# An attention and two-layer kernel on one core: the plain block's elementwise chain given to the scheduler ahead of other work, three steps' PSUM banks, and input differences on VectorE

## The chip, the cores and the metric

The kernel runs on one core of a Trainium2 chip. The metric is the device time of one execution in microseconds (us); the kernel before has been timed three times, and a profiled execution was taken besides. Engines are named as in the profile: PE is TensorE (PEld its weight loads), ACT is ScalarE, DVE is VectorE, POOL is GpSimd, SP is the engine that only issues transfers. A small q behind a name (SPq) marks the engine's queue of issued transfers and waits.

## What is computed

Three layers follow one another on 2304 tokens of width 512. The attention has 4 batches, 8 heads, 576 positions and 64 columns a head, half of the heads with a local mask and half with a strided one. Cut to what matters:

```python
x = attention(q, k, v)                    # (2304, 512)
h = x @ w_in                              # first block, 512 -> 2048 -> 512
x = (h - tanh(h)) @ w_out
rms = sqrt(mean(x * x) + 1e-6)            # second block, 512 -> 1536 -> 512
xn = x / rms * rms_g
g, val = xn @ w_gate, xn @ w_val
out = (silu(g) * val) @ w_out2
```

## The kernel before, in words

**Numbers in two parts.** Every float32 matrix is split into a high part that TensorE takes in its fp32r form and the rest as a low part, and each product is three matmuls: high by high, high by low, low by high. A split is two instructions: a copy (ACT), which rounds to the high part, and a subtraction (DVE), which gives the low part. Weights arrive as 64-bit words in tiles called `raw`, and are turned into float32 by ACT (L184 and L186) and a merge on DVE (L196, tile `ct`), and then split: copy L203 on ACT, subtraction L207 on DVE.

**Order of work.** Attention and the first block share the first 460 us: units of `pe_h`, tanh, `pe_x`, and attention in between. The last of the five token groups of the first block carries the conversion of the second block's first 18 weight tiles. Its result is evacuated by `evac_x` (ACT, L890) to DRAM.

The second block is done in two manners. The first 256 tokens (R0) are *plain*: for each of 12 slices f of the 1536 columns, `pe_gv(0, f)` does a gate group and a val group of 12 matmuls each (256 columns, output tiles `ps_h` and `ps_m`), then silu on ACT (L934), the product on DVE (L935), and the split of the product p: copy on ACT (L937), subtraction on DVE (L938). Two slices later `pe_o` multiplies p by the slice's w_out2 (6 matmuls) and adds to two banks of `ps_x`. While this goes on, the remaining weights are loaded, converted and stored to DRAM for later, so the block is both a computation and the preparation of the next.

The other 2048 tokens go through stages in two rounds of 1024 (j), with a pair of slices to a stage (p). There the work of a 2x2 block product is done with 7 products in place of 8, over sums and differences of the inputs (`conv`, tiles `xt`) and of the weights (`Decode`, POOL, lines L302, L285, L286). `conv(m)` makes one of seven inputs: for four of them a difference is formed first (`comb`, L1024, on POOL, 128x1024), and then it is split (copy L1043 on ACT, subtraction L1044 on DVE). For the first round the `conv` calls stand in the plain block, together with the end of the RMS norm (`prep_s`, L966 to L1010), which advances through a generator, three steps to a slice. For the second round they stand in the last stage of the first.

**What sets the order.** A scheduler orders the instructions of each engine before the run, by priority (the order in which the program issues them) and by its own estimate of when each can start. Every engine then takes its instructions in that order, and waits where one is not ready. Two things are fixed by hand: SP's transfers in the second block stand in program order, and so do PE's matmuls after the plain block. In the plain block PE's order is the scheduler's.

**Banks.** PSUM has eight tiles of 128x512 here: `ps_h` h0 and h1, `ps_m` m0 and m1, and four of `ps_x`. In the plain block steps alternate between h0 and h1 for the gate and m0 and m1 for the val. The norm's sum `ps_r` (read by ACT at L995) takes a tile of `ps_m` too. `pe_o` holds two of `ps_x` until the block ends. In the stages after it, the first products take h0, h1, m0 and m1, and `ps_q` and `ps_o` take `ps_x`.

**The loop of the plain block**, for each f: `st2.to(...)` loads and converts weights ahead (load L175 into three `raw` tiles, L184 to L207), `store.plain` and `store.to` store them (L343: `v<-ct`, L362: `w<-w`), `pe_gv(0, f)`, three steps of the generator, `decode.to(...)` from f = 5 on, and `pe_o(0, f - 2)`.

Of the kernel before, what the change touches and what calls it, by code (L numbers as in the profile page):

```python
# [7 lines left out]
F32 = mybir.dt.float32  # L8
F32R = mybir.dt.float32r
# [4 lines left out]
ACTF = mybir.ActivationFunctionType  # L14
ALU = mybir.AluOpType
# [5 lines left out]
WS = 2.0 ** -8  # L21
# [13 lines left out]
def attn_moe_moe_kernel(  # L35
# [24 lines left out]
    nc = tc.nc  # L60
# [6 lines left out]
    scale = 1.0 / float(D) ** 0.5  # L67
# [13 lines left out]
    def runs(s):  # L81

        r = []
        for i, (b, t) in enumerate(subs[s]):
            if r and r[-1][0] == b and r[-1][1] + r[-1][2] == t:
                r[-1][2] += 64
            else:
                r.append([b, t, 64, 64 * i])
        return r
# [36 lines left out]
    for s in range(len(subs)):  # L126
        if len(runs(s)) > 1 or s in LANES:
            _, t0, n, _ = runs(s)[0]
# [6 lines left out]
    def nth(tag, n):  # L135

        turn[tag] = (turn.get(tag, -1) + 1) % n
        return f"{tag}{turn[tag]}"
# [7 lines left out]
    def bank_x(name):  # L146
        return ps_x.tile([128, 512], F32, tag="x", name=name)

    def mm(out_, lhsT, rhs, start, stop):
        nc.tensor.matmul(out_, lhsT, rhs, start=start, stop=stop, skip_group_check=True)  # L150
# [182 lines left out]
    class Store:  # L333


        n = m = 0
# [586 lines left out]
    def pe_gv(j, f):  # L923
        r, n = [], R0
        for kd, pool, tag in (("gate", ps_h, "h"), ("val", ps_m, "m")):
            ps = pool.tile([128, 512], F32, tag=nth(tag, 2), name="ps_" + tag)[:, :n]
            w, x = w2[kd, f].t, xn[j]
            seq = [(a, e, c) for c in range(4) for a, e in ((0, 0), (0, 1), (1, 0))]
            for i, (a, e, c) in enumerate(seq):
                mm(ps, w[:, a, c, :], x[:, e, c, :], i == 0, i == len(seq) - 1)  # L930
            r.append(ps)
            if kd == "gate":
                s = pb.tile([128, n], F32, tag="s", name="s")
                nc.scalar.activation(out=s, in_=ps, func=ACTF.Silu, scale=WS)  # L934
        nc.vector.scalar_tensor_tensor(out=s, in0=r[1], scalar=WS, in1=s, op0=ALU.mult, op1=ALU.mult)  # L935
        t = pb.tile([128, 2, n], F32R, tag="p", name="p", bufs=3)
        nc.scalar.copy(out=t[:, 0], in_=s)  # L937
        nc.vector.tensor_tensor(out=t[:, 1], in0=s, in1=t[:, 0].bitcast(F32), op=ALU.subtract)  # L938
        p_of[j, f] = t

    def pe_o(j, f):
# [74 lines left out]
    def conv(m):  # L1016

        x = xt["raw"]
        b = {(k, h): x[:, 2 * k:2 * k + 2, HT * h:HT * (h + 1)] for k in range(2) for h in range(2)}

        def comb(name, p, q, out=None):
            if out is None:
                out = tmp[0].tile([128, 2, 512], F32, tag="w", name="tr")[:, :, :HT]
            nc.gpsimd.tensor_tensor(out=out, in0=p, in1=q, op=ALU.subtract)  # L1024
            xt[name] = out
            return out

        if m == 1:
            v = b[0, 0]
        elif m == 2:  # L1030
            v = b[1, 0]
        elif m == 3:
            v = b[1, 1]
        elif m == 5:
            v = comb("t1", b[0, 1], b[0, 0])
        elif m == 6:
            v = comb("t2", b[1, 1], xt.pop("t1"))
        elif m == 7:
            v = comb("t3", b[1, 1], b[0, 1])
        else:  # L1040
            v = comb("t4", b[1, 0], xt["t2"], xt["t2"])
        t = xt[m]
        nc.scalar.copy(out=t[:, 0], in_=v)  # L1043
        nc.vector.tensor_tensor(out=t[:, 1], in0=v, in1=t[:, 0].bitcast(F32), op=ALU.subtract)  # L1044
# [310 lines left out]
    pb = poolB.enter_context(tc.tile_pool(name="pb", bufs=2, reuse_waits="tile"))  # L1355

    for f in range(FB):
        if f == FB - 4:
            pairs[0].fetch((0, 1))
        st2.to(max(3 * (f + 2), N1 + (len(w2_order) - N1) * (f + 1) // (FB - 2)))  # L1360
        store.plain(st2.i - 1)
        store.to(st2.i - 6)
        pe_gv(0, f)
        for _ in range(3 if f < FB - 2 else 40):
            next(pg, None)
        decode.to(max(0, min(8, 8 * (f - 4) // 6)))
        if f > 1:
            pe_o(0, f - 2)
# [155 lines left out]
```

## Time and profile before

| what | value |
|---|---|
| median of three runs | 894.25 us (894.15 to 897.34) |
| profiled execution | 893.28 us |
| its span in the trace | 891.5 us |
| granted clock over the span | 0.99 |
| busy: PE, DVE, ACT, POOL | 97%, 71%, 46%, 30% |

The span runs from the first to the last instruction of the program; the profiled execution's own time includes what lies around it. Busy shares are means over parts with different limits, so the table of stretches among the rows below is read beside them. A matmul's end is modelled, so two groups may overlap by a little in the list of instructions; the distance between their starts is the better measure. An entry like "4.8 <-ACT s L934" names the idle time and what ended it.

### The profile page before, as it was taken

How to read it: one execution, taken by the hardware profiler on the slowest of the kernel's cores; microseconds unless marked ns; L12 is line 12 of the kernel's file. 1: busy time of each engine (PE TensorE's matmuls, PEld its weight loads, DVE VectorE, ACT ScalarE, POOL GpSimd, SP SyncE). 2: the span in 40 equal slices, each digit the busy share in tenths (PEclk: the TensorE clock that was granted, in tenths of full speed). 3: DMA queues.
4: the chain of work that ended last, by engine and by line, in shares of the span. 5: the costliest groups of instructions: out<-in, count | busy, mean ns of one | idle time of the engine just before them, and what ended most of it. 6: DMA issues, size and time to landing. Idle time of an engine off the chain costs nothing.

```text
span 891.5 us, 14064 instructions
## 1 busy us (share of the span) xinstructions
PE 866.0 (97%) x5091; PEld 723.4 (81%) x5091; DVE 633.5 (71%) x1282; ACT 413.3 (46%) x915; POOL 271.0 (30%) x317
## 2 busy tenths in 40 slices
PE   6999999999999999999988899999999999999998
PEld 3888888888998887888877887888788888888886
DVE  5999788888689896658869935469678553435544
ACT  6887643233444234868767534533325324322230
POOL 0000147694285952000003759846213000000000
PEclk9999999999999999999998999999999999999999
DMA  9964224311313102899958699865562189544002
GB/s 323 352 223 171 78 78 143 110 49 42 109 59 103 42 1 88 302 323 384 408 182 309 230 340 379 318 230 213 201 202 69 57 319 358 187 145 139 1 1 94
DMA packets 63750, 164.12 MB, mean 184 GB/s; under 512 B 10113, under 2 KB 21761, under 8 KB 63681
## 3 DMA queue, kind: packets, MB, share of 16 engines
q1 hardware_dynamic: 62528, 162.18, 51.6%
q10 hardware_dynamic: 1152, 1.05, 0.4%
q8 instruction: 40, 0.66, 0.3%
q14 instruction: 30, 0.24, 0.1%
HBM read 119.16 MB, written 44.04 MB: 183 GB/s over the span
## 4 chain that ended last, share of the span: by engine, by line
PE 58%; DVE 10%; POOL 7%; issue 2%; ACT 2%; DMA 2%; SPq 0%; DVEq 0%; ACTq 0%; POOLq 0%
PE ps_pr L150 20%; PE ps_o L150 14%; PE ps_x L150 9%; PE ps_h L150 9%; POOL pr L674 5%; DVE so L714 4%; PE ps_q L150 4%; PE ps_m L150 1%; POOL pr L707 1%; DVE tg L859 1%; DVE g L870 1%; DMA w<-w 1%; DMA wt<-w 1%; POOL ws L302 0%; DVE sm L450 0%
## 5 line engine op out<-in xcount | busy, mean ns | idle before, releaser
L150 PE MATMUL ps_h<-xs,w 128*128 128x512 f32 (+1 forms) x984 | 214.3, 366 | 0.7 <-DVE tg L859 0.7
L150 PE MATMUL ps_x<-g,w 128*128 128x512 f32 (+1 forms) x984 | 214.5, 366 | 0.2 <-ACT g L865 0.2
L150 PEld LDWEIGHTS ps_h<-xs,w 128*128 128x128 f32 x984 | 169.9, 190 | 30.6 <-DVE tg L859 1.1
L150 PEld LDWEIGHTS ps_x<-g,w 128*128 128x128 f32 x984 | 168.4, 189 | 30.5 <-ACT g L865 0.6
L150 PE MATMUL ps_pr<-xt,wt 128*128 128x512 f32 x576 | 137.4, 390 | 1.5 <-DVE s L1084 0.5
L150 PE MATMUL ps_o<-wt,p 128*128 128x512 f32 x576 | 135.9, 389 | 0.0
L150 PEld LDWEIGHTS ps_pr<-xt,wt 128*128 128x128 f32 x576 | 107.7, 188 | 25.7 <-DVE v L1096 1.4
L150 PEld LDWEIGHTS ps_o<-wt,p 128*128 128x128 f32 x576 | 108.1, 188 | 22.5
L674 POOL TENSOR_TENSOR pr<-sk,sq 128x256 f32<-128x256 f32 (+2 forms) x101 | 82.7, 856 | 132.0 <-DMA sq<-in_q_str_dram 126.7
L865 ACT CAST g<-tg 128x512 fp32r<-128x512 f32 (+1 forms) x82 | 46.5, 567 | 100.5 <-DVE tg L859 100.4
L1103 ACT COPY u<-ps_pr 128x512 f32<-128x512 f32 x72 | 41.9, 587 | 102.4 <-PE ps_pr L150 102.4
L707 POOL TENSOR_TENSOR pr<-sv,se 128x288 f32<-128x288 f32 (+12 forms) x104 | 69.9, 695 | 56.4 <-DVE so L714 19.8
L1154 DVE SCALAR_TENSOR_TENSOR osum<-ps_o,osum 128x512 f32<-128x512 f32 x80 | 54.6, 687 | 26.5 <-PE ps_o L150 26.2
L714 DVE TENSOR_REDUCE so<-pr 128x16 f32<-128x272 f32 (+11 forms) x104 | 65.3, 653 | 8.5 <-POOL pr L707 8.1
L150 PE MATMUL ps_pr<-xt,wo 128*128 128x512 f32 x288 | 67.4, 389 | 0.0
L1024 POOL TENSOR_TENSOR tr<-x 128x1024 f32<-128x1024 f32 x4 | 11.8, 2948 | 176.1 <-DMA raw<-in_w_val_dram 140.8
L150 PEld LDWEIGHTS ps_pr<-xt,wo 128*128 128x128 f32 x288 | 54.1, 188 | 11.3
L870 DVE TENSOR_TENSOR g<-tg,g 128x512 fp32r<-128x512 f32 (+1 forms) x82 | 54.9, 671 | 10.4 <-ACT g L865 9.8
L196 DVE SCALAR_TENSOR_TENSOR ct<-ca,ct 128x512 uint32<-128x512 uint32 x68 | 49.1, 731 | 18.6 <-ACT ca L186 18.1
L859 DVE SCALAR_TENSOR_TENSOR tg<-ps_h,tg 128x512 f32<-128x512 f32 (+1 forms) x82 | 50.6, 619 | 14.9 <-ACT tg L854 14.8
L854 ACT ACTIVATE tg<-ps_h 128x512 f32<-128x512 f32 (+1 forms) x82 | 44.2, 541 | 36.2 <-PE ps_h L150 36.2
L207 DVE TENSOR_TENSOR w<-ct,w 128x512 fp32r<-128x512 f32 x68 | 49.5, 737 | 11.2 <-ACT w L203 11.2
(122 smaller groups left out, 1077.2 us busy)
## 6 DMA issues: line engine op xcount, KB each, us to landing
wt<-w SPq DMA_DIRECT2D x84, 512.0 KB, 4.5
w<-w SPq DMA_DIRECT2D x36, 512.0 KB, 6.8
raw<-in_w_out_dram SPq DMA_DIRECT2D x28, 512.0 KB, 6.4
w<-wo SPq DMA_DIRECT2D x24, 512.0 KB, 6.8
raw<-in_w_in_dram SPq DMA_DIRECT2D x16, 512.0 KB, 9.0
raw<-in_w_gate_dram SPq DMA_DIRECT2D x12, 512.0 KB, 7.6
raw<-in_w_val_dram SPq DMA_DIRECT2D x12, 512.0 KB, 7.1
v<-ct SPq DMA_DIRECT2D x24, 256.0 KB, 6.3
```

What stands on the lines that cost most here:

```text
L150: nc.tensor.matmul(out_, lhsT, rhs, start=start, stop=stop, skip_group_check=True)
L196: nc.vector.scalar_tensor_tensor(out=t, in0=self.a.bitcast(U32), scalar=3, in1=t, op0=ALU.logical_shift_left, op1=ALU.bitwise_or)
L207: eng.tensor_tensor(out=t[:, 1], in0=self.b, in1=t[:, 0].bitcast(F32), op=ALU.subtract)
L674: nc.gpsimd.tensor_tensor(out=pr, in0=self.k[:, a:e, :], in1=self.q[:, c - c0:c - c0 + 1, :].to_broadcast([128, e - a, D]), op=ALU.mult,)
L707: nc.gpsimd.tensor_tensor(out=pr, in0=self.v[:, 0:c + 1, a:e], in1=self.e[:, c - c0, 0:c + 1].unsqueeze(2).to_broadcast([128, c + 1, e - a ...
L714: pend.append(lambda: nc.vector.tensor_reduce(out=o[:, c - g0, a:e], in_=pr.rearrange("l c d -> l d c"), axis=AX.X, op=ALU.add))
L854: nc.scalar.activation(out=t, in_=h_of[g, f, a], func=ACTF.Tanh, scale=WS)
L859: nc.vector.scalar_tensor_tensor(out=t, in0=h_of.pop((g, f, a)), scalar=WS, in1=t, op0=ALU.mult, op1=ALU.subtract)
L865: nc.scalar.copy(out=t[:, 0], in_=t_of[g, f, a])
L870: nc.vector.tensor_tensor(out=t[:, 1], in0=t_of.pop((g, f, a)), in1=t[:, 0].bitcast(F32), op=ALU.subtract)
L1103: nc.scalar.copy(out=u, in_=x[kd])
L1154: nc.vector.scalar_tensor_tensor(out=o, in0=ps, scalar=WS, in1=o, op0=ALU.mult, op1=ALU.add)
```

## The change

In `pe_gv` the tiles of every third step (f = 2, 5, 8, 11) come from `ps_x`, not from `ps_h` and `ps_m`, and the counters of those two don't advance in that step. The silu, which was issued behind the gate group, is now issued behind both groups, and it, the product, the copy and the subtraction stand in a block of higher priority: the scheduler treats them as if they had been issued 400 places earlier. Tile `s` has three buffers in place of two. In `conv`, the difference of two inputs is formed on DVE in place of POOL; `conv` is used for both rounds, so eight instructions in all move, four in the plain block and four in the last stage of the first round.

```diff
@@ pe_gv @@
         for kd, pool, tag in (("gate", ps_h, "h"), ("val", ps_m, "m")):
-            ps = pool.tile([128, 512], F32, tag=nth(tag, 2), name="ps_" + tag)[:, :n]
+            if f % 3 == 2:
+                ps = bank_x("ps_" + tag)[:, :n]
+            else:
+                ps = pool.tile([128, 512], F32, tag=nth(tag, 2), name="ps_" + tag)[:, :n]
...
-            if kd == "gate":
-                s = pb.tile([128, n], F32, tag="s", name="s")
-                nc.scalar.activation(out=s, in_=ps, func=ACTF.Silu, scale=WS)
-        nc.vector.scalar_tensor_tensor(out=s, in0=r[1], scalar=WS, in1=s, op0=ALU.mult, op1=ALU.mult)
-        t = pb.tile([128, 2, n], F32R, tag="p", name="p", bufs=3)
-        nc.scalar.copy(out=t[:, 0], in_=s)
-        nc.vector.tensor_tensor(out=t[:, 1], in0=s, in1=t[:, 0].bitcast(F32), op=ALU.subtract)
+        with tc.high_priority(400):
+            s = pb.tile([128, n], F32, tag="s", name="s", bufs=3)
+            nc.scalar.activation(out=s, in_=r[0], func=ACTF.Silu, scale=WS)
+            nc.vector.scalar_tensor_tensor(out=s, in0=r[1], scalar=WS, in1=s, op0=ALU.mult, op1=ALU.mult)
+            t = pb.tile([128, 2, n], F32R, tag="p", name="p", bufs=3)
+            nc.scalar.copy(out=t[:, 0], in_=s)
+            nc.vector.tensor_tensor(out=t[:, 1], in0=s, in1=t[:, 0].bitcast(F32), op=ALU.subtract)
@@ conv, comb @@
-            nc.gpsimd.tensor_tensor(out=out, in0=p, in1=q, op=ALU.subtract)
+            nc.vector.tensor_tensor(out=out, in0=p, in1=q, op=ALU.subtract)
```

## Rows read from the trace of the kernel before

**Rows 1.** The page, part 1: busy time, share of the span, instructions of each engine.

```profile
PE 866.0 (97%) x5091; PEld 723.4 (81%) x5091; DVE 633.5 (71%) x1282; ACT 413.3 (46%) x915; POOL 271.0 (30%) x317
```

**Rows 2.** Stretches: length, busy PE, PEld, DVE, ACT, POOL, granted clock, DMA share, GB/s.

```profile
464.00:472.00 8.00, 1.70 (x13) 1.49 (x12) 7.00 (x10) 7.97 (x12) 0.00 (x0) 0.85 0.81 255
472.00:477.20 5.20, 5.00 (x26) 5.00 (x27) 4.36 (x10) 3.97 (x10) 0.00 (x0) 0.57 0.92 297
477.20:491.00 13.80, 13.80 (x96) 12.67 (x95) 13.39 (x15) 8.23 (x15) 7.39 (x3) 1.00 0.89 336
491.00:497.00 6.00, 3.67 (x16) 3.38 (x16) 6.00 (x9) 3.92 (x7) 0.62 (x1) 0.72 0.37 113
497.00:518.00 21.00, 21.00 (x149) 19.72 (x149) 17.51 (x21) 9.40 (x20) 20.33 (x16) 1.00 0.85 284
518.00:528.00 10.00, 9.05 (x47) 7.46 (x46) 2.54 (x5) 3.60 (x8) 1.60 (x2) 1.00 0.99 342
528.00:560.00 32.00, 31.05 (x136) 25.02 (x135) 15.70 (x19) 13.56 (x24) 30.80 (x34) 1.00 0.99 372
560.00:891.50 331.50, 327.36 (x1441) 269.84 (x1439) 196.07 (x269) 108.73 (x179) 57.19 (x51) 1.00 0.47 167
```

**Rows 3.** Who PE waited for, 450 to 640 us: total, times, longest.

```profile
PE ps_h L150 <- ACT s L934: 4.8, 1, 4.8
PE ps_x L150 <- DVE p L938: 2.3, 1, 2.3
PE ps_m L150 <- ACT acc L995: 1.7, 1, 1.7
```

**Rows 4.** PE in order of time: start, length, operation, count, idle before.

```profile
472.20 4.98 PE L150 MATMUL ps_h<-xn,w 128*128 128x256 f32 x24 [4.84 <-ACT s L934]
...
503.79 1.59 PE L150 MATMUL ps_h<-xn,w 128*128 128x256 f32 x12
505.22 1.60 PE L150 MATMUL ps_m<-xn,w 128*128 128x256 f32 x12
...
523.47 1.59 PE L150 MATMUL ps_m<-xn,w 128*128 128x256 f32 x12
```

**Rows 5.** ACT in order of time, 455 to 500 us.

```profile
460.68 1.09 ACT L890 ACTIVATE xe<-ps_x 128x512 f32<-128x512 f32 x2 [2.89 <-PE ps_x L150]
...
470.47 1.28 ACT L934 ACT_TABLE_LOAD   x1
```

**Rows 6.** DVE and POOL in order of time, 455 to 521 us.

```profile
466.73 1.22 DVE L1044 TENSOR_TENSOR xt<-x,xt 128x1024 fp32r<-128x1024 f32 x1
...
481.30 4.88 DVE L1010 SCALAR_TENSOR_TENSOR x<-x,gcol,sq 128x512 f32<-128x512 f32 x4
...
486.77 2.60 DVE L196 SCALAR_TENSOR_TENSOR ct<-ca,ct 128x512 uint32<-128x512 uint32 x1
489.30 3.41 DVE L1044 TENSOR_TENSOR xt<-x,xt 128x1024 fp32r<-128x1024 f32 x1
...
493.30 0.68 DVE L196 SCALAR_TENSOR_TENSOR ct<-ca,ct 128x512 uint32<-128x512 uint32 x1
...
500.45 2.55 DVE L207 TENSOR_TENSOR w<-ct,w 128x512 fp32r<-128x512 f32 x1
...
482.84 2.79 POOL L1024 TENSOR_TENSOR tr<-x 128x1024 f32<-128x1024 f32 x1 [140.85 <-DMA raw<-in_w_val_dram]
...
497.60 4.86 POOL L1024 TENSOR_TENSOR tr<-x,tr 128x1024 f32<-128x1024 f32 x1 [5.97 <-DVE xt L1044]
```

**Rows 7.** SP's waits (total, times, longest), then SP, ACT, DVE in order of time.

```profile
SPq L343 <- DVE ct L196: 16.9, 4, 6.4
...
511.43 0.46 SPq L175 DMA_DIRECT2D raw<-in_w_val_dram  x1
...
518.08 0.76 ACT L184 ACTIVATE ct<-raw,colf 128x512 uint32<-128x512 uint16 x1 [1.42 <-DMA raw<-in_w_val_dram]
...
520.83 0.69 DVE L207 TENSOR_TENSOR w<-ct,w 128x512 fp32r<-128x512 f32 x1 [0.69 <-ACT w L203]
```

## The prediction

> **What bounds the kernel now.** I read the busy shares first: TensorE (PE) is busy 97% of the span [rows 1], so only time in which PE stands still or runs slowly can be won. Next the table of stretches: between 464 and 497 us PE is busy 24.17 of 33 us and the granted clock is 0.85, 0.57 and 0.72 in three of the four stretches; from 497 to 518 and in 528 to 560 it is nearly always busy [rows 2]. That hole is the start of the plain block. Then PE's waits there: 4.8 us on the silu of L934, 2.3 on the low half of p (L938), 1.7 on the evacuation of the norm's sum (L995, releasing a ps_m bank) [rows 3]. Last, what the named engines did. Silu of step 0 is no long job: ScalarE (ACT) stood 2.89 us waiting for the first block's last result at 460.68, then did casts and weight work, and reached the silu's table load only at 470.47 [rows 5]. The reader should see a queue position, not a shortage of ACT. The 2.3 us on p is another kind: VectorE (DVE) is busy 19.39 of 19.8 us from 477.2 to 497 [rows 2], and long instructions stand there [rows 6].
>
> **What the hole is worth.** Idle: 4.8 + 2.3 + 1.7 = 8.8 us [rows 3]. Slow clock after the long wait: 24 gate matmuls took 4.98 us, while two groups of 12 start 1.43 us apart in the steady part (503.79 to 505.22), so 2.86 for 24 [rows 4]: 2.1 lost; the level is about half, that is 1.2 of 2.4 GHz. After the second wait the clock averaged 0.72 over 3.67 busy us [rows 2]; half of these at most are lost (1.8), I take 1.4. Sum 12.3 us, the upper end of any gain here.
>
> **The parts.** (a) *Chain first* (silu, product, cast, subtraction: 4 instructions in each of 12 steps, none new). Nothing becomes cheaper; the queue positions on ACT and DVE change. Silu 0 moves from 470.47 towards 464, ahead of two casts and weight work that have slack. Its 1.28 us table load [rows 5] moves with it and then lies before the L995 that holds the ps_m bank. So I let the 1.7 us wait stay; bounds are 0 (step 2's matmuls fill it) and 1.7 + 1.28 = 3.0. What is moved back on ACT and DVE is weight conversion, the norm and the xt splits; on SP the stores of converted weights, and the raw loads queued behind them, follow the conversions.
>
> (b) *Banks for three steps.* Every third step takes two ps_x banks instead of one ps_h and one ps_m. Four ps_x banks are released by the first block's evacuation, which starts at 460.68 [rows 5], and the plain block's own sum needs two. So step 2's two groups (2 x 1.43 = 2.86 us) need no longer wait for silu 0. For the 4.8 us wait, (a) and (b) cover each other. The third s buffer adds no work. After the block, the next product groups take ps_h and ps_m, and ps_q takes ps_x banks: step 11 also uses ps_x, but ps_q's first use comes after the last p of the block is summed, so this wait costs nothing.
>
> (c) *Differences by DVE.* Four subtractions of 128x1024 leave POOL, four arrive at DVE, in this block and again in the stage behind it. The trace has none on DVE; the nearest row is the xt split, the same shape with two SBUF inputs, 1.22 us [rows 6]: 4 x 1.22 = 4.9 us added (bounds 4.9 alone, and 3.41 each, 13.6, if POOL's other work stretched all four). What it removes: DVE instructions that overlap POOL's subtractions are stretched. Four scalings of 128x512 took 4.88 against 4 x 0.68 for the size; a merge 2.60 against 0.68; an xt split 3.41 against 1.22; a weight subtraction 2.55 against 0.69 [rows 6, 7]: 2.2 + 1.9 + 2.2 + 1.9 = 8.2 us. Net DVE -3.3 us. POOL's first and last of four take 2.79 and 4.86 us [rows 6]; POOL is at 30.80 of 32 us later [rows 2], with other work (decoding weights), which can now begin when its loads land. In the second place DVE is far from full (196 of 331 us after 560, PE 327 [rows 2]); 4.9 us lie beside PE's work at no cost, and at 4.9 us if that cover is gone.
>
> The Trainium skill bears on (c) from both sides. Perfetto Trace Analysis, section Optimizing Scalar/DVE Operations, says that offloading from a saturated DVE, even to GpSimd, may make sense; by that alone this change costs DVE 4.9 us. The same section warns that the two share a read port, and SBUF — State Buffer, section SBUF: two separate sides, calls that port an exclusive lock, held for the whole instruction, which a DVE instruction with two SBUF inputs also wants. The stretched rows agree with the lock: by it DVE gains 3.3 us.
>
> **What is late next.** With 1.7 us left standing PE would be 12.3 - 1.7 = 10.6 us ahead at the end of the block, so step 11's val group, which began at 523.47 [rows 4], could begin at 512.9. But its weights were ready only at 520.83 + 0.69 = 521.5; their raw load was issued at 511.43 and ACT took it at 518.08 after waiting for it [rows 7]. SP issues in order, and stood 16.9 us in stores that wait for DVE's merge L196 [rows 7]. So the last weights come earlier only as DVE and SP do. DVE's work up to 518 is 7.00 + 4.36 + 13.39 + 6.00 + 17.51 = 48.3 us of 54 [rows 2]. Less 3.3 of work, it ends 3.3 us earlier with the same idle time, and 3.3 + 5.7 = 9.0 with none. I take 6 us, near the middle, since both the stretched merges and the queue positions that made SP wait change. Then val 11 starts at about 515.5 instead of 523.47: 8.0 us gained. PE then stands some 2.6 us before it, as long as the 2.3 us wait that cost about 1.4 us of clock; I subtract 1.0 for part of that. **Gain 7.0 us.** The wait before the block's last sum (its chain is short of cover in both kernels) stays.
>
> After the block PE runs 31.05 of 32 us while DMA is at 0.99 of its share [rows 2]. A shift of 7 us asks the transfers to come 7 us earlier too; DMA was idle 8 x 0.19 + 5.2 x 0.08 + 13.8 x 0.11 + 6 x 0.63 + 21 x 0.15 = 10.4 us between 464 and 518 [rows 2]. So it fits, barely, and a gain near 10 would not hold to the end.
>
> The profiled execution took 893.28 us with a span of 891.5, 1.8 outside it; it is 1.0 below the median of 894.25. 893.28 - 7.0 = 886.3, and at the median 887.2.
>
> **The rivals.**
> *Weights bound (24%).* The chain moves ahead, but weights come only by DVE's saved work, 3.3 us earlier; val 11 starts near 520, and PE gets to it sooner only to wait. For it: SP's waits, and transfers near their limit from 518 on. Against: DVE's 5.7 idle us up to 518 include waits that the change should shorten. Gain 3.3: 891.0.
> *The change doesn't do what it says (6%).* The order of each queue is laid out before the run from the scheduler's own estimates; the silu may already be as early as it thinks possible (its s tile lies in memory of the stage before). Then only the stretched DVE instructions go: 2.3 + 1.4 = 3.7 us, 890.6. Against: ACT's row at 470.47 stands behind work that nothing in the block's start waits for.
> *DVE stands in order (12%), slower.* A product placed at the head of DVE's queue while PE has yet to run the val group stops all behind it: merges, norm, xt splits, and through L196 SP. If DVE stood the whole group of 1.43 us and then 0.9 us through cast and back in each of 12 steps, that is 28 us on top of 50.8 - 3.3 = 47.5 us of work from 464 to 528 [rows 2]: 75.5 against 64, 11.5 us later, 905.7. It decides from (64 - 47.5) / 12 = 1.4 us of standing per step; my gain of 7 allows (57 - 47.5) / 12 = 0.8. For it: DVE is the fullest engine after PE. Against: from 497 to 518 the same in-order queue fed PE without a gap [rows 2]. The skill's advice to take work off a saturated DVE points the same way.
>
> **How the numbers follow.** Forecast 58%: gains of 4.5 to 12.3 us, 882 to 889.8; weights bound 24%; no effect of the order 6%; DVE in order 12%. About 0.5% (4.5 us) is what a measurement of this kernel can tell from no change. Faster: the 58 and a part of the weights case, 0.62; same: the rest of it, the 6 and the mild end of the last rival, 0.28; slower: 0.10. The range goes from the full 12.3 (882, and a little for the spread of runs) to 894.5, which leaves the slower rival out. Predicted 887.2.
>
> **What would show it.** Right: silu 0 near 464 to 466, no 4.8 us wait, clock above 0.9 throughout, no POOL subtraction of 128x1024, DVE merges at 0.7 us where POOL rests, val 11 near 515, and the time after the block as long as before. Wrong: a new PE wait on weights (w, L207) longer than 4 us, DVE waits on ps_m in every step, PE waits on transfers in the first stage after the block, or a longer first gap because of the table load. If val 11 starts earlier but the end doesn't, the transfers took it back.

## The result, and the profile after

The changed kernel takes 886.57 us (median of six runs, 883.68 to 889.58); the kernel before, run beside it, 894.79 (six runs, 892.87 to 897.34). The ratio is 0.9905, with a 95% interval of 0.9878 to 0.9933: 8.2 us less, against the 7.0 forecast. The profiled execution has a span of 884.8 us against 891.5, 6.7 less. Line numbers behind the edited function are three higher now: silu L937, product L938, copy L940, subtraction L941, difference L1027, xt copy and split L1046 and L1047.

Who PE waited for, 440 to 640 us, in the changed kernel (total, times, longest):

```profile
PE ps_m L150 <- ACT w L203: 1.6, 1, 1.6
PE ps_h L150 <- ACT s L937: 1.5, 1, 1.5
PE ps_x L150 <- ACT p L940: 1.2, 2, 1.0
PE ps_m L150 <- DVE w L207: 0.9, 2, 0.5
```

Of the three waits of [rows 3], those on the low half of p and on the norm's bank are gone, and the one on silu has shrunk from 4.8 to 1.5 us. The 2.5 us on weights (L203 and L207) weren't there before. The stretches of the changed kernel, with the columns of [rows 2], show where each lies:

```profile
464.00:472.00 8.00, 6.55 (x54) 6.35 (x54) 6.89 (x12) 7.93 (x13) 0.00 (x0) 1.00 0.90 285
472.00:480.00 8.00, 8.00 (x59) 7.57 (x58) 7.44 (x15) 7.49 (x17) 0.00 (x0) 1.00 0.89 294
480.00:497.00 17.00, 17.00 (x118) 15.72 (x117) 17.00 (x27) 11.48 (x21) 0.00 (x0) 1.00 0.90 313
497.00:520.00 23.00, 19.00 (x109) 15.52 (x108) 16.00 (x18) 9.13 (x17) 18.27 (x16) 1.00 0.90 322
```

The hole at the block's start has closed: from 464 to 497 PE is busy 31.55 of 33 us at clock 1.00 throughout, against 24.17 at as little as 0.57 [rows 2]. At the block's end, where PE had been full up to 518, 4.0 of 23 us are now idle. So the time won early is in part given back late. DVE is busy 17.00 of 17 us from 480 to 497.

PE's own list, in order of time, at both ends of the block:

```profile
463.84 1.72 PE L150 MATMUL ps_h<-xn,w 128*128 128x256 f32 x13
465.39 3.04 PE L150 MATMUL ps_m<-xn,w 128*128 128x256 f32 x24
469.88 3.14 PE L150 MATMUL ps_h<-xn,w 128*128 128x256 f32 x24 [1.45 <-ACT s L937]
...
511.56 2.89 PE L150 MATMUL ps_pr<-xt,wt 128*128 128x512 f32 x12
516.04 0.50 PE L150 MATMUL ps_m<-xn,w 128*128 128x256 f32 x2 [1.58 <-ACT w L203]
517.06 1.44 PE L150 MATMUL ps_m<-xn,w 128*128 128x256 f32 x10 [0.53 <-DVE w L207]
519.46 1.67 PE L150 MATMUL ps_x<-w,p 128*128 128x512 f32 x6 [0.95 <-ACT p L940]
520.97 2.90 PE L150 MATMUL ps_pr<-xt,wo 128*128 128x512 f32 x12
```

24 gate matmuls take 3.14 us after the short wait, where they took 4.98 after the long one [rows 4]. Val 11 begins at 516.04 (before: 523.47) and waits twice for its own weights. The group at 520.97 is the first that is wholly of the stage behind the block; before it began at 527.52. From there to the end of the span it is 363.83 us, and was 363.98: what the block gained is kept.

**A measure for the experiments.** The block's start, the last 28 `ps_x` matmuls of the first block, isn't touched by any kernel here (455.46 us before, 455.57 after; only silu 0 moves ahead of it, in two kernels), yet over all the profiled executions it lies anywhere from 453.65 to 459.46; why is told at the end. So beside the medians I give the *block*, from that start to the first group of the stage behind (527.52 and 520.97 above): 72.06 us before, 65.40 after. The time from there to the end was 363.2 to 364.3 us in all kernels. Each block is read from one profile. Each ratio is to the kernel before, run beside (893.68 to 895.31 us).

### The profile page after: what moved, and what is told of

Read it like the earlier page. It is cut to its first block, busy times and chain, and to the rows that moved or that the text cites. A ratio compares the mean times of both kernels' runs of the same rounds, so it can differ in the third digit from the quotient of the medians.

```text
span 884.8 us, 14060 instructions
## 1 busy us (share of the span) xinstructions
PE 862.6 (97%) x5091; PEld 719.3 (81%) x5091; DVE 628.9 (71%) x1290; ACT 413.4 (47%) x915; POOL 248.8 (28%) x309
## 3 DMA queue, kind: packets, MB, share of 16 engines
q10 hardware_dynamic: 1152, 1.05, 0.4%
## 4 chain that ended last, share of the span: by engine, by line
PE 57%; DVE 12%; POOL 7%; issue 2%; ACT 2%; DMA 1%; ACTq 0%; SPq 0%; DVEq 0%; POOLq 0%
PE ps_pr L150 19%; PE ps_o L150 14%; PE ps_x L150 9%; PE ps_h L150 9%; POOL pr L674 5%; DVE so L714 4%; PE ps_q L150 3%; PE ps_m L150 1%; POOL pr L707 1%; DVE tg L859 1%; DVE g L870 1%; DMA raw<-in_w_val_dram 1%; DVE s L1087 1%; DVE osum L1157 0%; DVE sm L450 0%
## 5 line engine op out<-in xcount | busy, mean ns | idle before, releaser
L302 POOL TENSOR_TENSOR ws<-wa 128x256 f32<-128x256 f32 x24 | 23.8, 1010 | 176.4 <-PE ps_h L150 155.7
L207 DVE TENSOR_TENSOR w<-ct,w 128x512 fp32r<-128x512 f32 x68 | 47.7, 710 | 9.7 <-ACT w L203 9.7
```

The costliest lines, as they stand in the source:

```text
L207: eng.tensor_tensor(out=t[:, 1], in0=self.b, in1=t[:, 0].bitcast(F32), op=ALU.subtract)
```

## The experiments

**The parts alone.** The first two kernels put one part into the kernel before, the third takes the priority out of the changed kernel.

Banks for three steps, and the third s buffer:

```diff
+            if f % 3 == 2:
+                ps = bank_x("ps_" + tag)[:, :n]
+            else:
...
-                s = pb.tile([128, n], F32, tag="s", name="s")
+                s = pb.tile([128, n], F32, tag="s", name="s", bufs=3)
```

> The kernel before with the banks part alone: every third step in ps_x, s in three buffers; silu in its old place, priority as before, differences on POOL. Theory (the priority moves nothing; the hole closes through the banks): the 4.8 us wait on silu 0 shrinks to under 2 us and the clock stays near full there; the stretched DVE instructions stay. The first product of the stage after the block (m = 5), at 527.5 us before and 521.0 after the change, starts at 522 to 525; 889 to 892 us. Rival (the priority opened the hole, banks are only cover): silu 0 and the wait stay above 4 us, 893 to 895 us.

Measured: 891.68 us, ratio 0.9975 (0.9955 to 0.9994); block 68.53, 3.5 less than before. PE's waits in it (440 to 640 us):

```profile
PE ps_x L150 <- DVE p L941: 2.5, 3, 1.1
PE ps_h L150 <- ACT s L937: 1.5, 1, 1.5
PE ps_m L150 <- ACT w L203: 1.3, 1, 1.3
PE ps_x L150 <- ACT p L940: 1.0, 1, 1.0
...
PE ps_m L150 <- DVE w L207: 0.7, 2, 0.5
```

The banks alone close the hole: the wait on silu is 1.5 us, as in the changed kernel, and the one on L995 is gone. But of that gain about half is lost again to waits on p and on weights.

Differences on VectorE:

```diff
-            nc.gpsimd.tensor_tensor(out=out, in0=p, in1=q, op=ALU.subtract)
+            nc.vector.tensor_tensor(out=out, in0=p, in1=q, op=ALU.subtract)
```

> The kernel before with the four differences on DVE alone. Theory: the 4.8 us wait on silu 0 stays, the 2.3 us wait on p goes with the stretched DVE instructions; m = 5 starts at 524 to 526, 890.5 to 892.5 us. Rival (DVE is full there, so the 4.9 us that it takes over cost more than the stretching did): 895 to 899 us, with new PE waits on DVE.

Measured: 889.18 us, ratio 0.9942 (0.9921 to 0.9963); block 67.53, 4.5 less than before. PE in order of time, and then its waits:

```profile
470.39 4.63 PE L150 MATMUL ps_h<-xn,w 128*128 128x256 f32 x24 [4.84 <-ACT s L934]
```

```profile
PE ps_m L150 <- ACT acc L995: 1.7, 1, 1.7
PE ps_x L150 <- ACT p L937: 1.0, 1, 1.0
```

The hole stands as it was; the 2.3 us on p [rows 3] are gone. The time lies below both expectations.

The changed kernel without priority:

```diff
-        with tc.high_priority(400):
...
+            if kd == "gate":
+                s = pb.tile([128, n], F32, tag="s", name="s", bufs=3)
+                nc.scalar.activation(out=s, in_=ps, func=ACTF.Silu, scale=WS)
```

> The changed kernel with silu back behind the gate group and the chain at its ordinary priority; banks and differences as changed. Theory (the priority moves nothing): every engine has the same order of instructions as the changed kernel, so the same time, 885 to 888 us, m = 5 at 521.0. Rival, as the prediction had it (chain first shortens the wait on silu 0 and the later waits on p): 2 to 5 us slower than the changed kernel, 889 to 891 us.

Measured: 885.57 us, ratio 0.9905 (0.988 to 0.993), as with the priority; block 64.11. Laid side by side, the two programs have the same instructions in the same order on PE, DVE, ACT, POOL and SP. So the priority moves nothing here, and the two profiles are two executions of one program: 65.40 and 64.11 say that a block's length is repeated to about 1.3 us.

The priority alone, in the kernel before:

> The kernel before with the high-priority block alone: no banks, two s buffers, differences on GpSimd. Theory (what holds silu 0 is the memory its tile lies in, not its priority): the wait of 4.8 us on silu 0 stays within 0.3 us, 894 to 896. Rival (priority moves the chain ahead of the weight work where it can): that wait falls below 3 us, 890 to 892.

Measured: 894.23 us, ratio 1.0002 (0.9989 to 1.0015); block 72.34. One row of PE's list tells it:

```profile
472.42 5.49 PE L150 MATMUL ps_h<-xn,w 128*128 128x256 f32 x24 [4.85 <-ACT s L934]
```

Here some neighbours on ACT do change places, but silu 0 doesn't move. Unlike what is said above, the kernel that ran has three `s` buffers, as the change has. So neither the priority nor the third buffer moves silu 0; in the banks kernel it is the banks that do.

**Which part brings the last weights.** SP's last two stores ahead of the last raw weight load, in the kernel before, the changed one, with the banks alone and with the differences alone:

```profile
499.02 10.33 SPq L343 DMA_DIRECT2D v<-ct  x2
```

```profile
496.93 6.12 SPq L343 DMA_DIRECT2D v<-ct  x2
```

```profile
498.00 8.85 SPq L343 DMA_DIRECT2D v<-ct  x2
```

```profile
494.41 6.52 SPq L343 DMA_DIRECT2D v<-ct  x2
```

The load behind them is issued 55.97, 49.60, 54.38 and 49.46 us after the block's start. So the differences bring it 6.5 us earlier and the banks only 1.6. The banks let PE come early, and the differences let the weights come early.

**What holds silu 0.** Its tile `s` lies over memory that the stage before it uses: in both programs silu 0's table load is the next instruction that ACT begins (at 470.47 before and 468.15 after) once the last subtraction that reads a `ct` tile of that stage has ended. That subtraction, before and after:

```profile
469.60 0.69 DVE L207 TENSOR_TENSOR w<-ct,w 128x512 fp32r<-128x512 f32 x1
```

```profile
466.84 0.68 DVE L207 TENSOR_TENSOR w<-ct,w 128x512 fp32r<-128x512 f32 x1
```

The changed kernel, with `s` in a pool of its own:

```diff
-            s = pb.tile([128, n], F32, tag="s", name="s", bufs=3)
+            s = pbv.tile([128, n], F32, tag="s", name="s")
...
+            pbv = ctx.enter_context(tc.tile_pool(name="pbv", bufs=2, side="right", reuse_waits="tile"))
```

> The changed kernel with s in memory of its own (two buffers), so that no tile of the stage before lies in its place. Theory: what held silu 0 was not its priority but the memory of s; now the table load and silu 0 stand ahead of the first block's last evacuation, before 461 us, the remaining 1.5 us wait on silu goes, and m = 5 starts 1 to 2 us earlier if the last weights don't hold it: 884.5 to 886.5 us. Rival (the block's end is set by its last weights): silu 0 is early, the 1.5 us wait goes, and the waits on weights (L203, L207) grow by as much: 886 to 887.5 us, m = 5 at 520.5 to 521.5.

Measured: 885.98 us, ratio 0.9911 (0.9886 to 0.9937); block 64.98. ACT in order of time, changed kernel first, then this one:

```profile
466.13 2.00 ACT L1046 CAST xt<-x 128x1024 fp32r<-128x1024 f32 x2
468.15 1.28 ACT L937 ACT_TABLE_LOAD   x1
469.45 0.94 ACT L937 ACTIVATE s<-ps_h 128x256 f32<-128x256 f32 x3
```

```profile
453.41 1.28 ACT L937 ACT_TABLE_LOAD   x1
455.55 0.38 ACT L937 ACTIVATE s<-ps_h 128x256 f32<-128x256 f32 x1 [0.85 <-PE ps_h L150]
```

With memory of its own silu 0 goes 14 us earlier (15 counted from the block's start), and PE never waits for it. The time is the same. The waits are now others:

```profile
PE ps_x L150 <- ACT p L940: 2.4, 2, 1.4
PE ps_m L150 <- DVE w L207: 1.3, 2, 1.1
...
PE ps_m L150 <- ACT w L203: 0.9, 1, 0.9
```

The waits on weights did not grow by what was won, as the rival had it (2.2 us, 2.5 before); those on p did. So in the changed kernel the block's start no longer sets its length; what comes late in the block does.

**What sets the end.** The last raw weight load (val 11) is issued by SP behind stores that wait for DVE, because the last 7 of its 36 steps load only one ahead. The changed kernel with the loads three ahead to the end:

```diff
     st2 = Stream(
...
-        3, 2 * FA, lambda i: True,
+        3, 3 * FA, lambda i: True,
```

> The changed kernel with one number altered: the look-ahead of the raw weight loads falls to one load at a point that lies a third of the list later, so the last loads keep running three ahead. Theory (the block's end is now set by the last weights, whose raw load was issued at 505.17 and whose gate and val groups waited 2.7 us on L203 and L207): that load is issued several us earlier, the waits on L203 and L207 at the block's end go to under 0.5 us, the stage after the block starts 2 to 3 us before 520.97, and the time is 883 to 885. Rival (DVE and the p chain bound the end, or the extra load only takes bandwidth from others): the wait only moves to p or to another transfer, the stage after the block starts within 1.5 us of 520.97, and the time is 886 to 888.

Measured: 883.53 us, ratio 0.9868 (0.9851 to 0.9884), 2.0 and 3.0 us below the two medians of the changed program (885.57 and 886.57), 3.3 by the ratios; block 60.82, 3.3 to 4.6 less. The stage behind starts at 520.28, only 0.7 us before 520.97, but this profile's block began 3.9 us later. The load of val 11 on SP, first in the changed kernel, then here:

```profile
505.17 0.43 SPq L175 DMA_DIRECT2D raw<-in_w_val_dram  x1
```

```profile
499.99 0.38 SPq L175 DMA_DIRECT2D raw<-in_w_val_dram  x1
...
512.30 1.46 PE L150 MATMUL ps_h<-xn,w 128*128 128x256 f32 x10 [0.20 <-DVE w L207]
...
514.88 1.46 PE L150 MATMUL ps_m<-xn,w 128*128 128x256 f32 x10 [0.41 <-DVE w L207]
516.17 2.91 PE L150 MATMUL ps_pr<-xt,wt 128*128 128x512 f32 x12
518.92 1.52 PE L150 MATMUL ps_x<-w,p 128*128 128x512 f32 x6
```

The load goes 5.2 us earlier (9 us counted from the block's start), the waits on weights shrink to 0.6 us, and val 11 now stands ahead of the first `ps_pr` group, which covers the 0.95 us that the last sum had waited for p in the changed kernel and in the one before. Its median is the lowest of all kernels here.

Both, own memory for `s` and the early loads:

> The changed kernel with both: tile s in memory of its own, and the last raw loads three ahead. If each of the two is held up by what the other removes (silu 0 at the block's start, the last weights at its end), the two together give more than either: the stage after the block starts 4 to 6 us before 520.97, 881 to 883. If the p chain on DVE bounds the block, own memory gives nothing again and the time is that of the early loads alone within 1 us, or 886 when those give nothing either.

Measured: 884.37 us, ratio 0.9877 (0.9861 to 0.9894); block 62.58. Nothing is added: PE gets to the later steps sooner and waits there for p (1.3 us on L940, 1.1 on L941).

The early loads in the kernel before:

> The kernel before with the last raw loads three ahead, nothing else. Theory (before, the block's end was set by the hole at its start and by DVE, and PE found the last weights just in time): 893 to 896, within 0.3% of the kernel before; the wait of 4.8 us on silu 0 stays. Rival (the last weights bounded the kernel before as well): 2 us or more faster, 892 or less.

Measured: 892.46 us, ratio 0.9972 (0.9961 to 0.9983); block 71.0, 1.1 less; the 4.8, 2.3 and 1.7 us stand unchanged. The median lies between the two expectations; against the 895.31 of the kernel before, run beside it, it is 2.85 us less: more than the 2 us that the rival asked for, and still within the 0.3% of the theory. So the run doesn't decide between them. Of the block's 1.1 us, 0.95 is the last sum's wait for p, covered here too by the new place of val 11. The rest of the 2.85 the one profile doesn't show.

**Do the parts add up?** Banks gave 3.5 us of block and differences 4.5, together 6.7 (7.95 in the other profile of the changed program). If the parts overlap, and the last weights are why, each should keep its own once the loads are early.

> The kernel before with the banks for three steps (and the third s buffer) and the last raw loads three ahead; the differences stay on GpSimd. Theory (banks and differences gave 3.5 and 4.5 us of block time alone and 6.7 together, because the last weights set the block's end, so with early loads each should keep its own): the missing differences now cost their full share, the block takes 5 to 7 us more than the 60.8 of the changed kernel with early loads, 888 to 890. Rival (the two overlap for another reason, in DVE's queue): 3 to 4 us more, 886 to 887.5.

> The kernel before with the differences on VectorE and the last raw loads three ahead; no banks. Theory: the hole at the block's start (4.8 us of wait on silu 0, 1.7 on the norm's bank, slow clock behind them) is now paid in full, the block takes 4 to 7 us more than 60.8, 888 to 890. Rival (PE makes up the hole later because something else still bounds the end): within 3 us of 60.8, 884 to 886.

Measured: banks and early loads 887.29 us, ratio 0.9924 (0.9909 to 0.9939), block 67.62; differences and early loads 889.18, ratio 0.9945 (0.993 to 0.9961), block 66.28. In one table, block in us:

| | neither | banks | differences | both |
|---|---|---|---|---|
| loads as before | 72.06 | 68.53 | 67.53 | 65.40 (again: 64.11) |
| last loads early | 71.0 | 67.62 | 66.28 | 60.82 |

With early loads the banks are worth 5.5 us where the differences are on VectorE (66.28 to 60.82), against 2.1 to 3.4 without (67.53 to 65.40 and 64.11). The differences are worth 6.8 where the banks are (67.62 to 60.82), against 3.1 to 4.4. The early loads give 3.3 to 4.6 to both parts together and 0.9 to 1.3 otherwise. So the blocks point to the last weights as what cut the two parts' sum. The times don't show it. By the ratios, banks and differences give 2.2 and 5.2 us alone and 8.5 together, so nothing is cut; the early loads give 2.5 us to the kernel before, 4.6 to the banks, nothing to the differences and 3.3 to both; and each of these steps is uncertain by 1 to 3 us. The step from banks and early loads to all three is 5.0 us by the ratios, 3.8 by the medians (the rival's figure), and 6.8 by the blocks, whose starts differ by 5.5 us (453.93 and 459.46). That the parts overlap at all rests on the block of 65.40; with 64.11 they add up. It is not shown. What is shown is that each part keeps a gain beside the other and the early loads (banks 6.9, differences 5.0 us by the ratios). With differences and early loads the hole is paid in full, and no later wait of PE in the block is left that could shrink and make it up:

```profile
474.03 4.62 PE L150 MATMUL ps_h<-xn,w 128*128 128x256 f32 x24 [4.84 <-ACT s L934]
```

**What the move from GpSimd is worth, and why.** The changed kernel, and GpSimd forms every difference a second time, in four pieces of 128x256, into a tile that nothing reads:

```diff
             nc.vector.tensor_tensor(out=out, in0=p, in1=q, op=ALU.subtract)
+            for i in range(4):
+                u = slice(256 * (i % 2), 256 * (i % 2) + 256)
+                nc.gpsimd.tensor_tensor(out=dum, in0=p[:, i // 2, u], in1=q[:, i // 2, u], op=ALU.subtract)
```

> The changed kernel, and GpSimd forms each of the differences a second time into a tile that nothing reads (four instructions of 128x256 for each difference, 16 in the block and 16 in the stage behind). This adds work; the output is unaffected. Theory (the gain of moving the differences is that GpSimd no longer holds up DVE): DVE instructions beside these subtractions are stretched again (a 128x512 scaling at 1.0 us or more in place of 0.68, a merge at 1.5 to 2.6), and the stage after the block starts 2 to 4 us after 520.97; 888 to 891. Rival (the gain is that the differences are ready sooner, or stand elsewhere in the order): DVE's instructions keep 0.7 and 1.2 us, the block keeps its length, 885 to 887.

Measured: 896.55 us, ratio 1.0017 (1.0001 to 1.0032); block 75.62, 10.2 more than the changed kernel. DVE, POOL, PE and SP in order of time:

```profile
485.51 3.70 DVE L1013 SCALAR_TENSOR_TENSOR x<-x,gcol,sq 128x512 f32<-128x512 f32 x4
489.14 1.84 DVE L941 TENSOR_TENSOR p<-s,p 128x256 fp32r<-128x256 f32 x2
...
493.57 1.76 DVE L1050 TENSOR_TENSOR xt<-x,xt 128x1024 fp32r<-128x1024 f32 x1
...
486.48 4.21 POOL L1030 TENSOR_TENSOR dum<-x 128x256 f32<-128x256 f32 x4 [143.22 <-ACT w L203]
...
517.10 0.72 POOL L1030 TENSOR_TENSOR dum<-x,tr 128x256 f32<-128x256 f32 x1
...
503.55 2.50 PE L150 MATMUL ps_m<-xn,w 128*128 128x256 f32 x10 [4.08 <-DVE w L207]
...
513.69 0.45 SPq L175 DMA_DIRECT2D raw<-in_w_val_dram  x1
```

The same three on DVE in the changed kernel, while POOL rests:

```profile
481.54 0.42 DVE L941 TENSOR_TENSOR p<-s,p 128x256 fp32r<-128x256 f32 x1
481.88 2.73 DVE L1013 SCALAR_TENSOR_TENSOR x<-x,gcol,sq 128x512 f32<-128x512 f32 x4
...
487.87 1.21 DVE L1047 TENSOR_TENSOR xt<-x,xt 128x1024 fp32r<-128x1024 f32 x1
```

The direction is as the theory had it, and the time lies beyond it (888 to 891): GpSimd's instructions, though nothing uses what they write, stretch VectorE's again (scalings 0.68 to 0.92 each, an xt split 1.21 to 1.76, two subtractions of p 1.84 us for the pair, 0.42 for one). VectorE holds up GpSimd as well: a piece takes 0.72 us at best and 1.05 on average in the four at 486.48. The size is beyond what was expected (10.2 us of block, not 2 to 4). I had set the expectation by the net gain of the move, 3.3 us; but here VectorE keeps its four new subtractions *and* gets GpSimd's contention back, so the gross 8.2 us of the prediction would have been the nearer measure. Not all of the 10.2 can be put down to the stretching: the added instructions also changed the order of some others (PE no longer waits for silu 0), and the last raw load, behind stores that wait for VectorE, is issued 8.5 us later (513.69 against 505.17), so that waits on L207 come to 7.0 us, behind the longest of which PE ran slowly (10 matmuls in 2.50 us, against 1.44 at 517.06 in the changed kernel).

## Why the prediction was right, step by step

**What bounds, and the hole.** Right in place: only the plain block changed, and the hole closed almost wholly (31.55 of 33 us busy, clock 1.00). The slow clock behind the long wait went with the wait (4.98 us for 24 gate matmuls to 3.14, where the forecast had 2.1 us lost); the 1.4 us can't be read by itself.

**(a) Chain first: this step failed.** The forecast had silu 0 near 464 by its priority. It went from 470.47 [rows 5] to 468.15, still behind the xt casts, and not by its priority: the changed kernel without it is the same program, and the kernel before with it keeps its 4.85 us wait. The banks alone give the 2.4 us (silu's table load stands 12.58 us after the block's start in both the banks kernel and the changed one, 15.01 before). The reason is the one named under the rival "doesn't do what it says": the tile lies in memory of the stage before. That rival's time was wrong all the same (890.6), since it let the banks fall with the priority. It cost the total nothing, because the forecast had said that (a) and (b) cover each other, and (b) works alone: the 4.8 became 1.5. Even a silu that really goes first (own memory) changes nothing.

**The 1.7 us on the norm's bank: wrong.** The forecast let it stay, with 0 as its lower bound if step 2's matmuls fill it. They do, and it is gone: PE has 13 gate matmuls to do at 463.84, while ACT evacuates the sum, where it had one.

**(b) Banks.** Right. Step 2's groups fill the hole, and the later use of `ps_x` by `ps_q` costs nothing (363.83 against 363.98 behind the block).

**(c) Differences by DVE.** Right in its net and in most of its terms. Four new instructions of 1.21 to 1.22 us, as the xt split had said:

```profile
485.80 1.21 DVE L1027 TENSOR_TENSOR tr<-x 128x1024 f32<-128x1024 f32 x1
...
489.94 1.22 DVE L1027 TENSOR_TENSOR tr<-x,tr 128x1024 f32<-128x1024 f32 x1
```

The stretched instructions of [rows 6] came down: the scalings from 4.88 to 2.73, an xt split from 3.41 to 1.21. Over the block the ten merges came down by only 0.4 us (9.14 to 8.78; 7.28 in the other profile of the program), where 1.9 was taken for one. DVE's busy time in the block fell from 52.19 to 49.00 us, 3.2 less (46.83 and 5.4 less in the other), against 3.3. Alone the move gives 4.5 us of block, where the terms were 2.3 + 1.4 = 3.7. The differences of the second round cost nothing. Of the two rules of the Trainium skill, the one that the traces agree with is the lock (SBUF — State Buffer, section SBUF: two separate sides): the repeated differences on GpSimd stretched an xt split on VectorE by 0.55 us. Perfetto Trace Analysis, section Optimizing Scalar/DVE Operations, says of moves between the two engines that they "might not help"; here the move away from GpSimd helped, by 3.1 to 6.8 us of block, according to what else was done.

**Late next: right, and the step that set the number.** The last raw load went 6.3 us earlier, 511.43 [rows 7] to 505.17, where I took 6; val 11 began at 516.04, where I had 515.5; PE stood 1.58 + 0.53 = 2.1 us for it, where I had 2.6. The differences alone brought the load as early, so the step from DVE's relief to SP to the weights is right. That its size came out is in part luck: the 6 was taken near the middle of 3.3 and 9.0. That this was a bound and not a coincidence the early loads show (block 3.3 to 4.6 us less). The 1.0 us taken off for a slow clock wasn't lost: the clock is 1.00 from 497 to 520. So block and span gained 6.7 us each, and the forecast of 7.0 was right though (a) failed and the 1.7 went: both change when PE arrives at the last weights, and hardly when these come.

**Rivals.** *Weights bound* named the right bound, but with the weights only 3.3 us earlier; they came 6.3 earlier, since SP's stores waited less too (the last two ahead of the load took 6.12 us, and 10.33 before). *DVE stands in order* wasn't seen: nothing was moved to the head of DVE's queue, and in the whole block PE waited 1.2 us for p. *Transfers* took nothing back.

## What to carry to other kernels

Before a priority is trusted to move an instruction, look at what its output tile's memory was used for last: a tile that lies over an earlier stage's memory can't go before that stage's last reader, whatever its priority. When one hole is closed, forecast the gain by what is late next and not by the hole: here 12.3 us of hole gave 6.7, because the last weights came only 6.3 us earlier, and the cheapest further gain (2 to 3 us) was one number in the look-ahead of the loads. Price work on GpSimd by what VectorE's instructions beside it take, not by GpSimd's idle time.

## What the runs showed of the hardware

**The start of an execution varies more than this change's parts.** In two kernels that run the same instructions before the block, in the same order, it began at 453.65 us in one profile and at 459.46 in the other. Over the first 50 us the granted clock was 0.93 and 0.80. Stretches of the two (differences alone first, early loads second; columns as in [rows 2]):

```profile
20.00:30.00 10.00, 7.87 (x208) 6.82 (x192) 9.56 (x25) 9.54 (x34) 0.00 (x0) 1.00 1.04 346
```

```profile
20.00:30.00 10.00, 8.63 (x123) 6.91 (x121) 9.06 (x27) 8.12 (x30) 0.00 (x0) 0.56 1.04 335
```

From 20 to 30 us the one runs 208 matmuls at full clock, the other 123 at 0.56 of it, so mostly at the 1.2 GHz level. The other part of the difference is a wait of 2.1 us that only the second profile has, between 400 and 440 us. That is why single profiles were compared by their blocks and not by their spans.

**GpSimd and VectorE slow each other by the instruction.** The same 128x256 subtraction on GpSimd took 0.72 to 1.66 us in one execution, and the 128x1024 one 2.40 to 4.86 in the kernel before, against 1.21 to 1.22 for VectorE with GpSimd at rest (the first three in the changed kernel). The instructions named as stretched read two inputs from SBUF. VectorE's product (L935 before, L938 after), which reads one of its two from PSUM, took 0.41 to 0.43 us in every step of the kernel before, the changed kernel and the one with the repeated differences, also in steps in which GpSimd was busy all the while (six before, two in the changed kernel).
